# A new order of all work behind the third attention step, up to block 2

## The chip, the cores and the metric

The kernel runs on one core of one Trainium2 chip. The metric is device time in microseconds (us) of one execution; the time given is the median of three runs. A profile was taken of one further execution.

## The reference

Three stages follow one another: a retention attention (no softmax, a decay between positions), a gated expert layer, and a soft mixture of experts whose slots are a softmax over all tokens.

```
scores = scale * q @ k.T                       # 8 batches, 8 heads, 576 positions, 64 wide
attn = (scores * Dmat) @ v                     # Dmat: gamma_h ** (i - j) where i >= j
x = attn, heads side by side                   # 4608 tokens x 512
h = x @ moe_w_in                               # 512 x 2048
x = (h * sigmoid(1.702 * h)) @ moe_w_out       # 2048 x 512
logits = x @ phi                               # 32 slots
d = softmax of logits over tokens              # slot_input = d.T @ x
slot_out[e] = relu(slot_input[e] @ w1[e]) @ w2[e]
out = softmax of logits over slots @ slot_out
```

## The kernel before

The tokens go in 12 blocks of 384, and a block in three attention steps of 128 tokens; 36 steps in all, nine to a pair of sequences. Attention carries a running state in PSUM (St), so a step is made of three kinds of 64x64 matmuls: its outputs, what it adds to the state, and the scores of the next step. A block's tokens then meet 16 slices of the first expert matrix (M, twelve 128x128x384 matmuls each, three for every 128 of depth: high weight by high x, high weight by low x, low weight by high x), a gate on ACT (g), and a 32x32 transpose on DVE (t).

All engines work through their instructions in the order in which the program writes them (a manual schedule). Blocks 0 and 1 and the attention steps up to 8 are written out as a string START of tokens (lines 49 to 62), which line 827 runs one by one; blocks 2 to 11 follow in a loop. The tokens, each with its engine:

- SP (DMA issues): T load of a step (1 MB), W and O load of a slice of the first expert matrix and of the turned second one (0.5 MB each), C and K constants, N four DMAs that shuffle a quarter of half a block's transposed gates into the tile nat (line 412). N0 to N7 are block 0, N8 on are block 1.
- PE: B, A, P, Q, R products of attention (line 227; B scores alone, P outputs and scores, Q outputs, R states, A all three), D a matmul whose result nobody reads (line 569), M expert products (line 368), e the product of phi with two turned slices (line 336), L logits (line 419), lt and dp parts of the softmax, SG the sum over a block's tokens into the slots (line 479).
- ACT: ua and aa (line 304), h (the high part of a weight slice, line 323), g (line 378), xh (the high part of x, line 252).
- DVE: us, as (line 308), uc, ac (line 313), v (the low part of a slice, line 327), SC, SS, xs (lines 237, 241, 245), t (line 394), ed (line 340), xl of steps 0 to 2 (line 257).
- POOL: KN (line 233) and xl from step 3 on.

Within products(), own matmuls (states, then scores) and outputs are issued in turn, on different halves of the rows. Three PSUM tiles (tag "r") are shared by outputs, scores, e and SG; three (tag "h") by M and D. The raw slices W and O go through seven places, six of them the tile early_raw, which shares its room with nat: the first N can't start before the last raw slice of O has been read by its ac. An ac of slice i writes place i % 4 of a ring that e of slices i - 4 has read. SG0 needs all of N0 to N7 landed, and the part dp0 of the softmax. Step 2 was done as Q2 (outputs) and, two products later, R2 (states). The token G runs one gate instruction early; it read St and wrote into early_raw.

```
        for i in range(max(len(own), len(out_))):
            for what, turn in ((own, 0), (out_, 1)):
                if i < len(what):
                    o, w, a, b, p, j, first_ = what[i]
```

Of the kernel before, what the change touches and what calls it, by code (L numbers as in the profile page):

```python
# [12 lines left out]
AF = mybir.ActivationFunctionType  # L13
# [5 lines left out]
B, H, S, D = 8, 8, 576, 64  # L19
# [7 lines left out]
C = 64  # L27
# [7 lines left out]
NDC = DM // 128  # L35
# [11 lines left out]
PC = NP * CP  # L47

START = (
# [13 lines left out]
).split()  # L63

RAWS = 7
# [68 lines left out]
def tile_kernel(ctx, tc, qkv, w_in, w_turned, w_out, phi, w1, w2, consts, out):  # L134
# [52 lines left out]
    xh, xl = {}, {}  # L187
# [16 lines left out]
    def products(g, parts=("out", "state", "score")):  # L204

        n, cb = g + 1, g % NPB
        own, out_ = [], []
        if "out" in parts and g >= 0:
            t = packs[g]
            Op = Ops[g] = ps.tile([128, NP, NSEQ, C], F32, tag="r", name="Op", bufs=3)  # L210
            for p, j in pairs:
                if cb:
                    out_.append((Op, t, SS, QT, p, j, True))
                out_.append((Op, t, VN, SC, p, j, cb == 0))
        if "state" in parts and g >= 0 and (g == 0 or 0 < cb < NPB - 1):
            own += states(g)
        if "score" in parts and n < NSTEP:
            Sp = Sps[n] = ps.tile([128, NP, NSEQ, C], F32, tag="r", name="Sp", bufs=3)
            own += [(Sp, packs[n], KT, QT, p, j, True) for p, j in pairs]
        if "state" in parts and cb == NPB - 1 and 0 <= g < NSTEP - 1:  # L220
            own += states(n)
# [4 lines that stand above are left out]
                    for h, oh in ((lo, (lo, hi)[turn]), (hi, (hi, lo)[turn])):  # L226
                        pe.matmul(o[oh, p, j, :], w[h, a, p, j], w[h, b, p, j], start=first_, stop=True,  # L227
                                  skip_group_check=True)
# [133 lines left out]

    def expert_scores(n, fc):
        hp = hps[n, fc] = ps.tile([128, NB], F32, tag="h", name="hp", bufs=3)
        i = 0
        for dc in range(NDC):
            for a, b in ((0, xh), (0, xl), (1, xh)):
                pe.matmul(hp, wt[fc][:, a, dc, :], b[n][:, dc, :], start=(i == 0), stop=(i == 3 * NDC - 1))  # L368
                i += 1

    def gelu(n, fc):
        g, fl = divmod(fc, GF)
# [193 lines left out]
    def again():  # L566
# [9 lines left out]
        "aa": lambda i: bring_sign(f"O{i}"), "as": lambda i: shift_low(f"O{i}"),  # L576
        "ac": lambda i: join(f"O{i}", ring[:, i % 4]), "e": wp_product, "ed": wp_turn,
        "A": products, "B": lambda i: products(i - 1, ("score",)), "P": lambda i: products(i, ("out", "score")),
        "Q": lambda i: products(i, ("out",)), "R": lambda i: products(i, ("state",)),
        "KN": scale_keys, "SC": scale_scores, "SS": scale_state,  # L580
        "xs": scale_out, "xh": x_high, "xl": lambda i: x_low(i, dve if i < STEPS else pool),
        "M": lambda i: expert_scores(*divmod(i, NFC)), "g": lambda i: gelu(*divmod(i, NFC)),
# [5 lines left out]
    def step(x):  # L588
        if x == "C":
            sp.dma_start(cs, consts[:, 128:128 + NCS])  # L590
        elif x == "K":
            constants()
        elif x == "D":
            again()
        elif x == "G":
            act.activation(early_raw[0:1, 0, 0:1], St[0][0:1, 0, 0, 0:1], AF.Gelu_apprx_sigmoid)
        elif x == "Z":
            dve.tensor_copy(sum4r, st.pop("s4"))
        else:
            name = x.rstrip("-0123456789")  # L600
            what[name](int(x[len(name):]))
# [351 lines left out]
```

## Time and profile before

| | |
|---|---|
| median of 3 runs | 650.64 us (649.29 to 652.19) |
| profiled execution, its own time | 650.49 us |
| its span, first to last instruction | 648.6 us |
| PE busy | 626.7 us (97%) |
| DVE, ACT, POOL busy | 293.8, 216.7, 77.6 us |
| mean rate of DMA | 232 GB/s |
| granted TensorE clock | 0.994 of full |

The span is 1.9 us shorter than the execution's time. The busy share of PE says that it has work almost all the time, not that it works at its peak. START takes the first 120 us of the span.

### The profile page before, as it was taken

How to read it: one execution, taken by the hardware profiler on the slowest of the kernel's cores; microseconds unless marked ns; L12 is line 12 of the kernel's file. 1: busy time of each engine (PE TensorE's matmuls, PEld its weight loads, DVE VectorE, ACT ScalarE, POOL GpSimd, SP SyncE). 2: the span in 40 equal slices, each digit the busy share in tenths (PEclk: the TensorE clock that was granted, in tenths of full speed). 3: DMA queues.
4: the chain of work that ended last, by engine and by line, in shares of the span. 5: the costliest groups of instructions: out<-in, count | busy, mean ns of one | idle time of the engine just before them, and what ended most of it. 6: DMA issues, size and time to landing. Idle time of an engine off the chain costs nothing.

```text
span 648.6 us, 19162 instructions
## 1 busy us (share of the span) xinstructions
PE 626.7 (97%) x8439; PEld 538.0 (83%) x8439; DVE 293.8 (45%) x581; ACT 216.7 (33%) x409; POOL 77.6 (12%) x70
## 2 busy tenths in 40 slices
PE   6999999999999999999999999999999999999994
PEld 6898788898998989989989979989898798874562
DVE  4989933364453443454534534544535323123043
ACT  2765432141242232422412412412424224231042
POOL 2011101211112101121111011111121100001000
PEclk9999999999999999999999999999999999999997
DMA  8997657687676756746657657566566777999998
GB/s 337 404 329 267 256 109 218 164 215 187 174 265 165 195 187 163 211 141 180 172 163 182 183 145 187 170 158 179 179 176 190 251 204 209 413 361 421 412 414 353
DMA packets 62546, 150.64 MB, mean 232 GB/s; under 512 B 8192, under 2 KB 42368, under 8 KB 53248
## 3 DMA queue, kind: packets, MB, share of 16 engines
q1 hardware_dynamic: 62464, 149.43, 72.8%
q8 instruction: 66, 1.08, 0.7%
q14 instruction: 16, 0.13, 0.1%
HBM read 101.16 MB, written 13.63 MB: 177 GB/s over the span
## 4 chain that ended last, share of the span: by engine, by line
PE 87%; DMA 6%; DVE 3%; ACT 1%; issue 1%; POOL 0%; SPq 0%; DVEq 0%; ACTq 0%
PE hp L368 56%; PE Lg L419 5%; PE Sg L479 4%; PE Sp L227 4%; PE St L227 4%; DMA early_raw<-in_moe_w_in_dram 3%; PE Op L227 2%; PE h_ps L710 2%; PE op L787 2%; PE so_ps L761 1%; DMA early_raw<-in_w_turned_dram 1%; PE so_ps L753 1%; DMA ring<-in_w_turned_dram 1%; DMA pack<-in_qkv_dram 1%; PE tpg L401 1%
## 5 line engine op out<-in xcount | busy, mean ns | idle before, releaser
L368 PE MATMUL hp<-x,w 128*128 128x384 f32 x2304 | 420.0, 339 | 1.6 <-POOL x L257 1.3
L368 PEld LDWEIGHTS hp<-x,w 128*128 128x128 f32 x2304 | 397.4, 188 | 20.2 <-issue 15.7
L394 DVE STREAM_TRANSPOSE pre<-gT 128x384 f32<-128x384 f32 x172 | 95.3, 569 | 165.5 <-ACT gT L378 154.5
L378 ACT ACTIVATE gT<-hp 128x384 f32<-128x384 f32 x188 | 91.1, 490 | 232.6 <-PE hp L368 232.2
L257 POOL TENSOR_TENSOR x<-xs,x 128x512 fp32r<-128x512 f32 x33 | 42.5, 1288 | 310.6 <-ACT x L252 310.6
L227 PE MATMUL Op<-pack 64*64 64x64 f32 x2176 | 71.8, 220 | 0.2 <-issue 0.2
L227 PEld LDWEIGHTS Op<-pack 64*64 64x64 f32 x2176 | 66.8, 135 | 0.6 <-issue 0.6
L252 ACT CAST x<-xs 128x512 fp32r<-128x512 f32 x36 | 22.3, 620 | 87.5 <-DVE xs L245 87.4
L233 POOL TENSOR_TENSOR pack<-pack,cs 128x512 f32<-128x512 f32 x30 | 32.2, 1072 | 126.9 <-DMA pack<-in_qkv_dram 111.3
L227 PE MATMUL Sp<-pack 64*64 64x64 f32 x1152 | 41.3, 222 | 5.6 <-DMA pack<-in_qkv_dram 5.5
L227 PEld LDWEIGHTS Sp<-pack 64*64 64x64 f32 x1152 | 37.8, 138 | 8.1 <-DMA pack<-in_qkv_dram 5.5
L237 DVE TENSOR_TENSOR pack<-Sp,cs 128x512 f32<-128x512 f32 x36 | 24.7, 686 | 33.5 <-PE Op L227 25.8
L227 PEld LDWEIGHTS St<-pack 64*64 64x64 f32 x1024 | 33.2, 137 | 7.4 <-issue 7.3
L227 PE MATMUL St<-pack 64*64 64x64 f32 x1024 | 37.4, 224 | 0.0
L419 PE MATMUL Lg<-gT,Wp 128*32 128x384 f32 x376 | 36.3, 493 | 0.5 <-DVE Lall L466 0.5
L479 PE MATMUL Sg<-nat,dn 128*32 128x512 f32 x264 | 30.4, 593 | 0.0
L245 DVE TENSOR_TENSOR xs<-Op,cs 128x512 f32<-128x512 f32 x36 | 24.5, 681 | 3.1 <-PE Op L227 3.1
L241 DVE TENSOR_TENSOR pack<-St,cs 128x512 f32<-128x512 f32 x32 | 21.8, 680 | 3.4 <-PE St L227 2.0
L304 ACT ACTIVATE early_raw<-early_raw 128x512 f32<-128x512 f32 x28 | 18.9, 685 | 12.3 <-DMA early_raw<-in_moe_w_in_dram 6.3
L479 PEld LDWEIGHTS Sg<-nat,dn 128*32 128x32 f32 x264 | 8.4, 110 | 17.1 <-issue 16.9
L485 DVE SCALAR_TENSOR_TENSOR acc<-acc,corr,Sg 128x512 f32<-128x512 f32 x10 | 7.5, 748 | 28.1 <-PE Sg L479 28.1
L419 PEld LDWEIGHTS Lg<-gT,Wp 128*32 128x32 f32 x376 | 9.6, 109 | 11.9 <-issue 9.1
(142 smaller groups left out, 386.8 us busy)
## 6 DMA issues: line engine op xcount, KB each, us to landing
pack<-in_qkv_dram SPq DMA_DIRECT2D x36, 1024.0 KB, 6.2
nat<-pre SPq DMA_DIRECT2D x352, 96.0 KB, 2.2
wx<-in_moe_w_dram SPq DMA_DIRECT2D x19, 1024.0 KB, 11.2
ring<-in_moe_w_out_dram SPq DMA_DIRECT2D x16, 512.0 KB, 4.0
early_raw<-in_moe_w_in_dram SPq DMA_DIRECT2D x15, 512.0 KB, 6.7
early_raw<-in_w_turned_dram SPq DMA_DIRECT2D x13, 512.0 KB, 6.9
wx<-in_moe_w_dram SPq DMA_DIRECT2D x11, 512.0 KB, 10.1
out_dram<-wx SPq DMA_DIRECT2D x5, 1024.0 KB, 7.5
```

The lines of the kernel that those rows point to most:

```text
L227: pe.matmul(o[oh, p, j, :], w[h, a, p, j], w[h, b, p, j], start=first_, stop=True, skip_group_check=True)
L233: (dve if n in (3, 4) else pool).tensor_tensor(k, k, by_state(ksc[:, n % NPB, :]), op=ALU.mult)
L237: dve.tensor_tensor(packs[n][:, SC], Sps.pop(n), across(dtab), op=ALU.mult)
L241: dve.tensor_tensor(packs[n][:, SS], St[n // NPB], by_state(stsc[:, n % NPB, :]), op=ALU.mult)
L245: dve.tensor_tensor(xss[g], Ops.pop(g), across(osc), op=ALU.mult)
L252: act.copy(xh[b_][:, :, i * CP:(i + 1) * CP], xss[g].rearrange("p a j c -> p a (j c)"))
L257: (eng or pool).tensor_tensor(xl[b_][:, :, cols_], xss.pop(g).rearrange("p a j c -> p a (j c)"), xh[b_][:, :, cols_], op=ALU.subtract)
L368: pe.matmul(hp, wt[fc][:, a, dc, :], b[n][:, dc, :], start=(i == 0), stop=(i == 3 * NDC - 1))
L378: act.activation(gT[n, g][:, fl, :], hps.pop((n, fc)), AF.Gelu_apprx_sigmoid)
L394: dve.transpose(pre[n, hf][:, :, :, fh, :].rearrange("p c b i -> p (c b) i"), gT[n, g][:, fl, :].rearrange("p (x j) -> p x j", j=32))
L419: pe.matmul(Lg[n][32 * fl:32 * fl + 32, :], Wp[:, g * GF + fl, :], gT[n, g][:, fl, :], start=(g == 0), stop=(g == NFC // GF - 1))
L479: pe.matmul(Sg[32 * b:32 * b + 32], dn[n][:, c, :], nv[:, 4 * b:4 * b + 4], start=(c == 0), stop=(c == NT128 - 1))
```

## The change

The string START holds the same tokens in another order, with one exception: Q2 and R2 become one token S2, so that step 2's outputs and states are issued in turn. Every load, every DVE, ACT and POOL instruction and every matmul stays. What moves: S2 and the scores B3 stand ahead of M0, with two D ahead of S2 and one behind B3; W0 and W1 stand behind T2 as before, but G no longer holds them, since it now reads and writes gate_room (set by a memset on POOL); the transposes t and the slices O stand in another order; e, L, products and softmax parts stand in longer runs between the M's; N0 stands behind T7 and is followed by T8; SG0 and A8 stand three M's earlier against the rest. The very first expert product, M0, takes its twelve matmuls by terms: four of high weight by high x, four of low weight by high x, four of high weight by low x.

```diff
--- before.py
+++ after.py
@@ -47,19 +47,19 @@
 PC = NP * CP
 
 START = (
-    "T0 C T1 T2 B0 KN0 SC0 R0 G SS1 P0 KN1 W0 W1 R1 SC1 T3 W2 xs0 W3 KN2 SS2 P1 xh0 W4 W5 xl0 SC2 T4 ua0 W6 xs1 Q2 D "
-    "D D us0 ua1 us1 xh1 uc0 xs2 h0 xl1 xh2 v0 xl2 W7 uc1 h1 ua2 M0 KN3 v1 us2 ua3 R2 g0 uc2 h2 W8 us3 M1 v2 ua4 uc3 "
-    "us4 h3 ua5 uc4 W9 M2 g1 v3 h4 us5 W10 SS3 KN4 K ua6 B3 v4 g2 uc5 W11 ua7 M3 us6 h5 us7 uc6 ua8 v5 h6 uc7 W12 M4 "
-    "g3 v6 h7 us8 O0 ua9 v7 ua10 uc8 W13 M5 g4 SC3 h8 us9 ua11 v8 uc9 ua12 W14 M6 Z us10 g5 us11 h9 uc10 aa0 v9 h10 "
-    "A3 uc11 O1 T5 g6 v10 h11 us12 O2 ua13 us13 v11 M7 ua14 SC4 W15 SS4 uc12 aa1 M8 uc13 g7 us14 h12 xs3 h13 uc14 xh3 "
-    "v12 M9 g8 v13 O3 h14 us15 as0 ua15 v14 aa2 M10 uc15 g9 as1 h15 as2 ac1 ac0 A4 T6 g10 as3 aa3 O4 ac2 O5 ac3 O6 "
-    "M11 v15 O7 SC5 KN5 O8 SS5 O9 xl3 xs4 g11 t0 M12 xh4 as4 aa4 t1 xl4 aa5 t2 t3 e1 e0 ed1 g12 as5 as6 M13 aa6 ed0 "
-    "ac5 aa7 as7 ac4 ac7 g13 ac6 M14 t4 KN6 t5 t6 aa8 as8 L0 A5 xs5 t7 g14 xh5 xl5 t8 aa9 as9 t9 M15 t10 T7 O10 t11 "
-    "O11 SC6 O12 e2 SS6 g15 O13 e3 O14 t12 ed2 M16 ac8 ed3 O15 ac9 t13 t14 g16 KN7 t15 M17 aa10 as10 ac10 aa11 as11 "
-    "g17 ac11 M18 aa12 as12 aa13 as13 L1 e4 g18 ed4 ac12 ac13 M19 e5 ed5 aa14 as14 ac14 aa15 as15 ac15 g19 M20 N0 e6 "
-    "g20 ed6 N1 M21 e7 g21 ed7 N2 M22 N3 L2 L3 g22 M23 sp0 lt0 g23 M24 t16 t17 A6 t18 t19 t20 t21 M25 T8 SS7 g24 N4 "
-    "N5 N6 N7 SC7 xs6 dp0 t22 g25 M26 xh6 t23 xl6 M27 g26 A7 g27 L4 L5 SS8 T9 SC8 M28 xs7 xh7 xl7 g28 M29 KN9 g29 M30 "
-    "SG0 A8 g30 M31 t24 xs8 t25 xh8 SC9 xl8 g31 t26 t27 t28 t29 t30 t31 N8 T10 N9 N10 N11 "
+    "G T0 C T1 B0 T2 KN0 SC0 R0 P0 KN1 KN2 SS1 R1 W0 xs0 SC1 SS2 W1 xh0 xl0 P1 ua0 D us0 SC2 xs1 uc0 ua1 D us1 xh1 "
+    "T3 S2 h0 uc1 xl1 xs2 xh2 B3 W2 W3 D W4 h1 ua2 ua3 v0 us2 xl2 v1 uc2 W5 W6 h2 W7 M0 g0 us3 uc3 h3 us4 ua4 M1 v2 "
+    "v3 uc4 M2 t0 us5 h4 v4 ua5 g1 g2 uc5 W8 M3 us7 us6 h5 ua6 v5 ua7 T4 W9 KN3 uc6 SS3 h6 uc7 M4 SC3 h7 v6 us8 ua8 "
+    "W10 g3 v7 g4 M5 g5 uc8 ua10 A3 M6 ua9 W11 us10 us9 xs3 M7 t1 h8 O0 ua11 O1 g6 us11 uc9 v8 h9 M8 v9 uc10 aa1 "
+    "W12 K h10 g7 uc11 W13 SS4 SC4 xh3 us12 T5 h11 v10 aa0 v11 W14 ua12 M9 KN4 ua13 M10 ua14 as0 g8 as1 ac0 us13 "
+    "W15 uc12 uc13 ac1 t7 A4 us15 h12 KN5 g9 us14 uc14 e0 h13 ua15 ed0 O2 v12 as2 aa2 O3 g10 SC5 v13 M11 O4 h14 g11 "
+    "aa3 M12 uc15 g12 as3 M13 xl3 v14 ac3 T6 h15 SS5 aa4 O5 ac2 O6 M14 xs4 O7 v15 e1 as5 O8 aa5 A5 Z aa7 O9 xh4 as4 "
+    "xl4 ac4 as7 aa6 M15 xs5 O10 ac5 xh5 ed1 ac7 O11 as6 ac6 g13 g14 O12 t2 e2 t4 t3 L0 g15 e3 t5 xl5 O13 as10 as11 "
+    "M16 O14 g16 M17 g17 aa8 as8 aa14 ac8 M18 O15 t8 g18 M19 as9 t11 T7 ed3 as13 ed2 M20 t14 SC6 as14 aa10 aa11 SS6 "
+    "t10 M21 aa12 KN6 as12 ac11 as15 g19 M22 t12 aa15 ac10 aa9 ac9 e5 t6 ac14 aa13 ac15 e4 L1 g20 ed4 e7 KN7 g21 "
+    "ed5 ac12 ac13 A6 ed7 SS7 M23 SC7 t15 M24 t9 t13 g22 M25 e6 g23 N0 xs6 T8 L2 ed6 g24 L3 N1 xh6 sp0 A7 lt0 M26 "
+    "xs7 xl6 N2 SS8 SC8 g25 N3 g26 M27 N4 M28 T9 N5 M29 t16 KN9 dp0 t21 t23 A8 N6 t17 t18 g27 t22 xh7 xs8 L4 N7 t19 "
+    "t24 g28 g29 t20 SG0 t27 xl7 N8 L5 t29 M30 xh8 T10 N9 N10 g30 M31 g31 xl8 t30 t28 SC9 N11 t26 t25 t31 "
 ).split()
 
 RAWS = 7
@@ -362,11 +362,11 @@
 
     def expert_scores(n, fc):
         hp = hps[n, fc] = ps.tile([128, NB], F32, tag="h", name="hp", bufs=3)
-        i = 0
-        for dc in range(NDC):
-            for a, b in ((0, xh), (0, xl), (1, xh)):
-                pe.matmul(hp, wt[fc][:, a, dc, :], b[n][:, dc, :], start=(i == 0), stop=(i == 3 * NDC - 1))
-                i += 1
+        terms = [(a, b, dc) for dc in range(NDC) for a, b in ((0, xh), (0, xl), (1, xh))]
+        if (n, fc) == (0, 0):
+            terms.sort(key=lambda x: x[0] + 2 * (x[1] is xl))
+        for i, (a, b, dc) in enumerate(terms):
+            pe.matmul(hp, wt[fc][:, a, dc, :], b[n][:, dc, :], start=(i == 0), stop=(i == 3 * NDC - 1))
 
     def gelu(n, fc):
         g, fl = divmod(fc, GF)
@@ -576,7 +576,7 @@
         "aa": lambda i: bring_sign(f"O{i}"), "as": lambda i: shift_low(f"O{i}"),
         "ac": lambda i: join(f"O{i}", ring[:, i % 4]), "e": wp_product, "ed": wp_turn,
         "A": products, "B": lambda i: products(i - 1, ("score",)), "P": lambda i: products(i, ("out", "score")),
-        "Q": lambda i: products(i, ("out",)), "R": lambda i: products(i, ("state",)),
+        "S": lambda i: products(i, ("out", "state")), "R": lambda i: products(i, ("state",)),
         "KN": scale_keys, "SC": scale_scores, "SS": scale_state,
         "xs": scale_out, "xh": x_high, "xl": lambda i: x_low(i, dve if i < STEPS else pool),
         "M": lambda i: expert_scores(*divmod(i, NFC)), "g": lambda i: gelu(*divmod(i, NFC)),
@@ -593,7 +593,8 @@
         elif x == "D":
             again()
         elif x == "G":
-            act.activation(early_raw[0:1, 0, 0:1], St[0][0:1, 0, 0, 0:1], AF.Gelu_apprx_sigmoid)
+            pool.memset(gate_room[0:1, 0:1], 0.0)
+            act.activation(gate_room[0:1, 1:2], gate_room[0:1, 0:1], AF.Gelu_apprx_sigmoid)
         elif x == "Z":
             dve.tensor_copy(sum4r, st.pop("s4"))
         else:
```

## Rows read from the trace of the kernel before

**Rows 1.** Page, parts 1 and 5: busy us, share, count; mean ns

```profile
PE 626.7 (97%) x8439; PEld 538.0 (83%) x8439; DVE 293.8 (45%) x581; ACT 216.7 (33%) x409; POOL 77.6 (12%) x70
...
L419 PE MATMUL Lg<-gT,Wp 128*32 128x384 f32 x376 | 36.3, 493 | 0.5 <-DVE Lall L466 0.5
```

**Rows 2.** Windows: length, busy PE, PEld, DVE, ACT, POOL, clock, DMA share, GB/s

```profile
60.00:80.00 20.00, 18.38 (x339) 15.63 (x338) 18.14 (x39) 9.57 (x18) 2.45 (x2) 1.00 0.68 256
```

**Rows 3.** Waits of PE, 0 to 125 us: total, times, longest

```profile
PE hp L368 <- POOL x L257: 1.3, 2, 0.9
PE wps L336 <- issue: 1.1, 1, 1.1
PE wps L336 <- DVE xs L245: 0.7, 1, 0.7
PE wps L336 <- DVE pack L237: 0.5, 1, 0.5
```

**Rows 4.** Timeline of PE, 13 to 32 us: start, us, line, tiles, count

```profile
13.14 3.07 PE L227 MATMUL Op<-pack 64*64 64x64 f32 x98 [0.24 <-issue]
16.14 2.20 PE L569 MATMUL again<-pack 128*128 128x384 f32 x6
...
18.80 2.18 PE L368 MATMUL hp<-x,w 128*128 128x384 f32 x11 [0.29 <-DVE x L257]
20.91 1.15 PE L227 MATMUL St<-pack 64*64 64x64 f32 x32
21.99 4.43 PE L368 MATMUL hp<-x,w 128*128 128x384 f32 x24
...
27.43 4.78 PE L368 MATMUL hp<-x,w 128*128 128x384 f32 x26
```

**Rows 5.** Timeline of PE, four M in a row; one M between two e

```profile
37.98 8.59 PE L368 MATMUL hp<-x,w 128*128 128x384 f32 x48
...
78.50 0.65 PE L336 MATMUL wps<-ring,phis 128*32 128x64 f32 x32
79.09 2.35 PE L368 MATMUL hp<-x,w 128*128 128x384 f32 x12
81.37 0.65 PE L336 MATMUL wps<-ring,phis 128*32 128x64 f32 x32
```

**Rows 6.** Window of the products A4 alone, columns as in rows 2

```profile
46.50:48.52 2.02, 2.02 (x129) 1.95 (x128) 0.00 (x0) 0.00 (x0) 1.64 (x2) 1.00 0.81 312
```

**Rows 7.** Timeline of SP, 81 to 109 us: N0-N3, T8, N4-N7, T9

```profile
81.74 11.33 SPq L412 DMA_DIRECT2D nat<-pre  x16
95.50 0.34 SPq L184 DMA_DIRECT2D pack<-in_qkv_dram  x1
95.88 12.75 SPq L412 DMA_DIRECT2D nat<-pre  x16
108.74 0.54 SPq L184 DMA_DIRECT2D pack<-in_qkv_dram  x1
```

**Rows 8.** Timeline of DVE: the last ac before N0

```profile
81.03 0.69 DVE L313 SCALAR_TENSOR_TENSOR ring<-early_raw 128x512 int32<-128x512 int32 x1
```

**Rows 9.** DMA, 81.7 to 108.7 us: instruction queue; issues, KB, us to landing

```profile
q8 instruction: 3, 0.05, 0.8%
...
nat<-pre SPq DMA_DIRECT2D x32, 96.0 KB, 2.8
```

**Rows 10.** Line 412, 78 to 130 us: duration of one issue, min/median/max ns

```profile
L412 SPq DMA_DIRECT2D nat<-pre x49: 585/598/1982, 81.7 to 129.9; - x49
```

**Rows 11.** Timeline of PE: SG0, then the first M of block 2

```profile
112.10 2.78 PE L479 MATMUL Sg<-nat,dn 128*32 128x512 f32 x24
...
119.80 8.42 PE L368 MATMUL hp<-x,w 128*128 128x384 f32 x47 [0.43 <-POOL x L257]
```

**Rows 12.** Timeline: an as on DVE beside an xl on POOL

```profile
67.53 1.42 DVE L308 TENSOR_SCALAR early_raw<-early_raw 128x512 int32<-128x512 int32 x1
...
67.39 1.27 POOL L257 TENSOR_TENSOR x<-xs,x 128x512 fp32r<-128x512 f32 x1 [8.04 <-ACT x L252]
```

## The prediction

> **What bounds the kernel now.** I read the page first: PE is busy 97% of the span [rows 1], so only two things can move the time, fewer or shorter pieces of PE work and idle time of PE. Next come the waits of PE in the stretch that START covers: behind the first landing they add up to some 3.6 us, 1.3 for the low part of x from POOL and 2.3 in three waits of the e products [rows 3]. From M1 to the end of the first logits there is no other idle time on PE that the waits name. DVE is the engine behind it: 18.14 of 20 us at 60 to 80 [rows 2]. What a busy PE hides is read from its timeline. Four M's in a row take 46.50 - 37.98 = 8.52 us (to the product that rows 6 begin with), an M between two e's 81.37 - 79.09 = 2.28 [rows 5]. With m for an M and s for a change to other work and back, 4m + s = 8.52 and m + s = 2.28, so m = 2.08 and s = 0.20. And step 2 costs its states twice over: the R2 row alone holds PE from 20.91 to 21.99, 1.08 us for 32 records, while A4 gets 128 records through in 2.02 us because two kinds alternate [rows 4, 6].
>
> **The change, part by part.** All work stays, so the sum is a new place for each piece on PE's line, and then a look at what is not ready there.
>
> The head. The row at 13.14 holds 98 records in 3.0 us, 34 of P1 and 64 of Q2, so Q2 starts at about 14.1 and takes 2.0; three D's take 2.05 (2.20 less the overlap of the last end) [rows 4]. P1 comes 0.1 later, since SC1 now stands behind xs0 on DVE. After the change PE runs from 14.2: two D's, S2, B3, one D, M0. S2 has 16 pairs of outputs and 8 of states, 96 records; by the alternation of A4 the states hide and it takes Q2's 2.0. So M0 starts at 14.2 + 2.05 + 2.0 + 1.1 = 19.4. It needs xs2, xh2 and v0: S2 ends at 17.6, and two operations of the 0.69 kind [rows 8] on end give 19.0; the low part of x comes later but M0 wants it only for its last four matmuls, that is what the order by terms is worth (0.3 us of waiting before [rows 4]). Three M's and a change later M3 starts at 25.7. Before it was 27.43 with the same work done [rows 4]: 1.7 us won, of which 1.08 is R2 hidden, 0.4 two changes less, the rest idle time. G's early start lets W0 and W1 leave SP some 7 us sooner, but they queue behind T2 all the same; I cost that at nothing, as M0 waits for x, not for W0.
>
> M3 to e5. Twenty M's at 2.08, A3 to A5 at 2.02 [rows 6], e0 to e3 at 0.59 (79.09 - 78.50) [rows 5], L0 at 36.3/47 = 0.77 [rows 1], and four and a half changes at 0.20: 41.6 + 6.1 + 2.4 + 0.8 + 0.9 = 51.8, so e5 starts at 77.5. The three old waits for e are gone by place: e0 follows A4 alone, with the ac of its slices moved forward on DVE, and e1 comes after M14 rather than M12. What is late next is block 1's x. On DVE, as6 and ac6 (for e3) now stand right beside xl4 and xl5 on POOL, and an as beside an xl has taken 1.42 us where its own length is near 0.4 [rows 12]; also aa7 and as7 stand ahead of xh4 and xs5, so one late slice of O delays x. Bounds: 0 if the slice lands in time, 1.0 to 1.5 if not. I take 0.5, nearer the low end since A5 itself comes two M's sooner against block 0. e5 then starts at 78.0. Before, it started at 78.50 with three M's fewer done [rows 5].
>
> e5 to SG0: here the gain is given back. ac14 must wait for e5 (the ring place that e5 reads), and ac14, ac15, ed4, ed5, ac12, ac13 stand in a row on DVE: 0.6 for e5, then four starts 0.60 apart and two ed of 0.2, so the last raw slice is read at about 81.6, and only then may N0 overwrite early_raw. Before, N0 started at 81.74, right behind the last ac at 81.03 [rows 7, 8]: the shuffles start no earlier than they did. They are 32 DMAs on SP that took 11.33 and 12.75 us; with T8 (0.34) and T9 (0.54) between them that is 24.96 [rows 7]. T8 no longer waits for A6 (2.4 us in the gap from 93.07 to 95.50 [rows 7]), since A6 is done at about 83. So N7 is issued by 106.6, and its last DMA, 0.6 from issue to issue and 2.8 from issue to landing [rows 9, 10], is there at 108.8. PE by itself would be at SG0 sooner. From e5's start: four e's 2.4, L1 to L4 3.1, A6 to A8 6.1, seven M's 14.6, lt0 and dp0 together 0.8 (an estimate, five matmuls beside M's 0.17 each), changes 0.5: 27.5, so 105.5. SG0 waits 3.3 us.
>
> [...] First the rows: one issue of line 412 has a median of 598 ns but went up to 1982, and three packets of the instruction queue fall into the stretch [rows 9, 10]; in the trace they lie at the long issues, so I take those for their price. [...]
>
> SG0 to block 2. SG0 2.7, L5 0.8, M30 and M31 with a change 4.3: block 2 starts at 108.8 + 7.8 = 116.6. Before it started at 119.80 less one matmul, 119.6, as the first M of block 2 waited 0.43 for xl8 [rows 11]; now SG0, L5, M30 and M31 lie between A8 and it, 7.8 us against the one M of before, and xl8 is there in time. Nothing behind START changes and PE has no stall there that isn't tied to PE's own progress, so I carry the difference to the end: 119.6 - 116.6 = 3.0 us. Against the profiled execution's own 650.49 us (0.15 under the median of the three, 650.64) this gives 647.4.
>
> **The rivals.**
>
> One: the shuffles aren't late. At the median issue of 0.60 and 0.04 between, 32 take 20.4; with T8 and T9 N7 would be issued by 102.9 and landed by 105.1, under the 105.5 at which PE comes. SG0 doesn't wait, 3.3 us more are won: 644.1. For it speaks that 0.60 is the usual issue [rows 10]; against it that both old stretches of 16 took 11.33 and 12.75, not 10.2 [rows 7]. Chance 0.2.
>
> Two: block 1's x and e3 are late by the upper bound and a little more (as6 behind POOL, one slice of O late). All that hangs on e5 moves with it, N0 too: 1.5 us more, 648.9. For it speaks rows 12, against it that A5, which x waits for, and M16 move forward together. Chance 0.2.
>
> Three, to the other side: SP's line of shuffles grows. T8 and T9 are now each followed closely by shuffles, and the packets of both share the same DMA engines; should the stretch grow past 24.96 by more than the 3.0 us won, the kernel gets slower. With four issues as long as the longest (4 x 1.4 over the median), and T8 and T9 each holding a later issue for 2 us, it is 20.4 + 0.9 + 5.6 + 4 = 30.9, SG0 starts at 114.7, and the time is 653.3. For it speaks the 12.75 of the stretch that had a T ahead of it against 11.33 without [rows 7], against it that it needs every issue at its worst. Chance 0.08.
>
> Four: the change doesn't do what it says, S2 doesn't hide the states, since only half of S2 alternates. Then 1.08 us come back ahead of everything: 648.5. Against it, P1 has the same shape and alternated. Chance 0.05.
>
> **How the numbers follow.** The forecast, 647.4, has the remaining 0.47, with a range of its own of 646 to 649 (the wait of x 0 to 1.5, the stretch of shuffles 1.2 either way). For the range I leave out half of rival three, the lower edge of rival one and little else: 643.8 to 650.4. Half a per cent, about what a measurement of this kernel can tell from no change, is 3.3 us, so the border of faster lies at 647.4, on the forecast itself. Faster: half of the forecast and rival one, 0.24 + 0.2, and a bit of the others, 0.46. Slower by as much takes 653.9, the far end of rival three: 0.04. The same: 0.5.
>
> **What would show it.** In the trace after: R2's row at 20.9 is gone and M3 starts near 25.7 (27.43 before); S2's 96 records take some 2.0; the e products carry no waits over 0.5 us; e5 starts near 78 behind M22; N0 on SP starts near 81.6, as before; SG0 has an idle time of about 3 us in front that a DMA of nat ended, and starts near 109; the first M of block 2 starts near 116.6 without waiting for POOL. SG0 without a wait shows rival one; a wait of M16 or e3 over 1 us rival two; N0 to N7 taking over 28 us rival three. The forecast is wrong as a whole if A3 or A4 waits: SC3 and the landing of T5 come closest ahead of them, and a wait there moves all behind it.

## The result and the profile after

The changed kernel takes 658.20 us, the median of six runs (656.89 to 658.92); the kernel before takes 650.36 in as many (649.29 to 652.19). The ratio is 1.0115, with a 95% interval of 1.0097 to 1.0133. The forecast was 647.4, the range 643.8 to 650.4: the kernel got 1.15% slower where I had given that 4 in 100. The profiled execution of after took 658.33 us, its span is 656.6.

First its page, part 1, as in [rows 1], and the waits of PE up to the end of START, as in [rows 3].

```profile
PE 626.7 (95%) x8439; PEld 538.5 (82%) x8439; DVE 294.5 (45%) x581; ACT 215.7 (33%) x409; POOL 79.2 (12%) x71
```

```profile
PE Sp L227 <- DMA pack<-in_qkv_dram: 6.8, 2, 5.7
PE Op L227 <- issue: 3.0, 2, 2.8
PE Sp L227 <- issue: 2.2, 2, 1.3
PE Sg L479 <- DMA nat<-pre: 2.1, 1, 2.1
PE wps L336 <- DVE ring L313: 1.9, 2, 1.6
PE hp L369 <- ACT gT L378: 0.6, 1, 0.6
```

PE is busy 626.7 us as before, to the tenth; that is a coincidence, as S2 hides R2's 1.08 us [rows 4] and a stretch at a granted clock of 0.50, shown below, makes other work longer. By the sums, the 7.9 us by which the span grew are idle time of PE. The largest part of that idle time, 3.0 + 2.2 us, has no engine and no DMA as its releaser: "issue", PE waiting for nothing that the profile shows. Where it arises is told by the starts of the first matmuls (us, read from the timeline of PE in both traces):

| | M0 | M3 | M16 | block 2 | block 3 | block 4 | end |
|---|---|---|---|---|---|---|---|
| before | 17.89 | 27.43 | 67.36 | 119.04 | 164.93 | 211.38 | 648.63 |
| after | 23.87 | 30.21 | 71.01 | 126.71 | 173.17 | 219.30 | 656.55 |
| later by | 5.98 | 2.78 | 3.65 | 7.68 | 8.25 | 7.92 | 7.92 |

From block 4 on the difference stands still. All but 0.24 us of it is made in START, most of it in two places: ahead of M0, and between M16 and block 2. (M3 is less late than M0, as R2 and B3 now stand ahead of M0.) The timeline of PE in after shows the first of these places (the same columns as [rows 4]; dots stand for rows of S2 and B3), and the windows show the clock granted there (the third column from the end).

```profile
15.80 1.68 PE L227 MATMUL Op<-pack 64*64 64x64 f32 x34 [2.83 <-issue]
17.41 2.69 PE L569 MATMUL again<-pack 128*128 128x384 f32 x4
...
20.97 1.35 PE L227 MATMUL Op<-pack 64*64 64x64 f32 x32
...
22.23 1.03 PE L227 MATMUL Sp<-pack 64*64 64x64 f32 x29
23.19 0.91 PE L569 MATMUL again<-pack 128*128 128x384 f32 x2
```

```profile
16.00:17.00 1.00, 1.00 (x31) 1.00 (x28) 0.00 (x0) 0.13 (x1) 0.00 (x0) 0.66 1.02 418
17.00:18.00 1.00, 1.00 (x10) 0.79 (x7) 0.48 (x1) 0.00 (x0) 0.00 (x0) 0.50 1.04 422
18.00:19.00 1.00, 1.00 (x3) 0.48 (x2) 1.00 (x3) 0.75 (x2) 0.00 (x0) 0.50 1.01 410
19.00:20.00 1.00, 1.00 (x3) 0.19 (x1) 0.90 (x3) 0.52 (x1) 0.00 (x0) 0.63 1.04 410
20.00:21.00 1.00, 1.00 (x65) 0.97 (x66) 0.55 (x1) 0.00 (x0) 0.00 (x0) 1.00 1.03 406
```

In the middle of P1 PE stands still for 2.83 us. Behind that the granted clock is 0.50 until between 19 and 20 us, and two D's take 2.69 us where [rows 4] has three in 2.20. From 15.80 to the first product of S2, at 20.03, PE needs 4.2 us for 34 products of P1 and two D's; at the pace of [rows 4] (98 products in 3.0 us, three D's in 2.05) it would be 2.4. So the pause costs 2.6 us more than before and the slow clock some 1.8. S2 follows and takes 2.1, from 20.03 to the first product of B3 at 22.12.

Now a view that tells what the "issue" is: windows that start at 0 and end just before PE goes on after each of these pauses. The brackets behind PE and PEld count the matmuls and weight loads that PE has started by then.

```profile
0.00:15.78 15.78, 7.32 (x222) 6.84 (x223) 4.82 (x8) 3.10 (x5) 3.42 (x8) 1.00 0.88 349
0.00:64.60 64.60, 54.25 (x986) 50.21 (x986) 45.69 (x86) 33.08 (x60) 6.06 (x10) 0.97 0.89 330
0.00:90.00 90.00, 77.53 (x1368) 71.21 (x1369) 65.91 (x126) 43.39 (x79) 11.84 (x14) 0.98 0.77 287
0.00:102.33 102.33, 88.93 (x1624) 81.11 (x1624) 69.70 (x133) 46.54 (x84) 13.11 (x15) 0.98 0.78 276
```

The sums of the two counts are 445, 1972, 2737 and 3248; the trace has 4, 13, 16 and 17 more instructions of PE by then that are not counted as busy (most of them semaphores). That makes 449, 1985, 2753 and 3265. So PE pauses behind its instructions 448, 1984, 2752 and 3264, give or take one: 192 plus 1, 7, 10 and 12 times 256. The page of after shows what comes in such pieces:

```profile
q8 instruction: 66, 1.08, 0.7%
```

66 packets of the instruction queue carry 1.08 MB, 16.4 KB each. In both traces they pair off one by one with PE's 66 entries into a piece, so I take this queue to bring PE's program. And each pause ends 2.3 to 2.9 us after such a packet starts (13.29, 62.32, 87.60 and 99.49 us in the trace of after). So my reading is that PE waits for its own program, and that the next piece is asked for at about the time when PE comes to the piece before. Where PE is at M's, 24 instructions each and 8.59 us for four [rows 5], 256 last over 20 us by my estimate; of the 64x64 products a step like A4 has 256, in 2.02 us [rows 6]. Before has the same pause in the same place, 0.24 us at instruction 448: it is the bracket in the first line of [rows 4], and I passed over it. The other "issue" of [rows 3], 1.1 us at an e, falls at instruction 1612 and 5.4 us after a packet, so it is no such pause; what ended it stays open.

The second place, from M16 on. First DVE and POOL around e3, then SP with N0, T8, N1 to N4, T9 and N5 to N8, to be laid beside [rows 7].

```profile
67.42 1.51 DVE L308 TENSOR_SCALAR early_raw<-early_raw 128x512 int32<-128x512 int32 x1
69.03 1.34 DVE L313 SCALAR_TENSOR_TENSOR ring<-early_raw 128x512 int32<-128x512 int32 x1
...
66.90 1.75 POOL L257 TENSOR_TENSOR x<-xs,x 128x512 fp32r<-128x512 f32 x1 [0.96 <-ACT x L252]
68.60 1.22 POOL L233 TENSOR_TENSOR pack<-pack,cs 128x512 f32<-128x512 f32 x1
```

```profile
89.28 3.29 SPq L412 DMA_DIRECT2D nat<-pre  x4
92.68 0.52 SPq L184 DMA_DIRECT2D pack<-in_qkv_dram  x1
93.26 13.43 SPq L412 DMA_DIRECT2D nat<-pre  x16
106.80 0.52 SPq L184 DMA_DIRECT2D pack<-in_qkv_dram  x1
107.36 17.78 SPq L412 DMA_DIRECT2D nat<-pre  x16
```

as6 takes 1.51 and ac6 1.34 beside xl5 and KN6 on POOL, where the medians of their groups are 0.42 and 0.68, and e3 waits 1.56 for them. N0 starts at 89.28, N7's last issue ends at 116.95; A8 waits 1.10 for T9, and SG0, after four of its 24 matmuls, 2.09 for the last shuffles.

### The profile page after: what moved, and what is told of

The parts are those of the page before. It is cut to its first block, busy times and chain, and to the rows that moved or that the text cites. A ratio compares the mean times of both kernels' runs of the same rounds, so it can differ in the third digit from the quotient of the medians.

```text
span 656.6 us, 19163 instructions
## 1 busy us (share of the span) xinstructions
PE 626.7 (95%) x8439; PEld 538.5 (82%) x8439; DVE 294.5 (45%) x581; ACT 215.7 (33%) x409; POOL 79.2 (12%) x71
## 3 DMA queue, kind: packets, MB, share of 16 engines
q8 instruction: 66, 1.08, 0.7%
## 4 chain that ended last, share of the span: by engine, by line
PE 87%; DMA 4%; DVE 3%; SPq 2%; issue 2%; ACT 1%; DVEq 0%; ACTq 0%
PE hp L369 56%; PE Lg L419 5%; PE Sg L479 4%; PE St L227 4%; PE Sp L227 4%; DMA pack<-in_qkv_dram 3%; PE Op L227 3%; PE h_ps L711 2%; SPq L412 2%; PE op L788 2%; DMA early_raw<-in_moe_w_in_dram 1%; PE so_ps L762 1%; PE so_ps L754 1%; DVE ring L313 1%; PE tpg L401 1%
## 5 line engine op out<-in xcount | busy, mean ns | idle before, releaser
L227 PE MATMUL Op<-pack 64*64 64x64 f32 x2176 | 73.5, 221 | 3.0 <-issue 3.0
L227 PEld LDWEIGHTS Sp<-pack 64*64 64x64 f32 x1152 | 37.9, 137 | 10.8 <-DMA pack<-in_qkv_dram 7.0
## 6 DMA issues: line engine op xcount, KB each, us to landing
wx<-in_moe_w_dram SPq DMA_DIRECT2D x19, 1024.0 KB, 13.5
```

## The experiments

Three causes were to be told apart: PE's own program (and with it the early W0 and W1, which are on the DMA queues when a packet is due, and S2, which puts more small matmuls in a row), the order of the tail (A8, SG0 and the shuffles), and e3 beside POOL. The ratio is to before in the same rounds. The last column is the difference to before of the first M of block 4, in the one profiled execution of each; it need not be a typical one (that of e2_free is the slowest of its eight, that of e8_late_e3 the fastest of its ten).

| run | us | ratio to before, 95% | block 4 |
|---|---|---|---|
| after | 658.20 | 1.0097 to 1.0133 | +7.92 |
| e1_hold | 657.82 | 1.0084 to 1.0141 | +5.84 |
| e2_free | 652.65 | 1.0014 to 1.0055 | +3.81 |
| e3_s2 | 653.69 | 1.0036 to 1.0068 | +3.10 |
| e4_late | 654.52 | 1.0046 to 1.0093 | +2.48 |
| e5_s2_fill | 656.60 | 1.0063 to 1.0124 | +4.10 |
| e6_late_qr | 657.43 | 1.0082 to 1.0144 | +4.79 |
| e7_after_fill | 660.72 | 1.0113 to 1.0198 | +9.81 |
| e8_late_e3 | 655.74 | 1.0062 to 1.0105 | +2.31 |
| e9_s2_quick | 652.76 | 1.0036 to 1.0061 | +1.62 |
| e10_before_quick | 651.63 | 1.0010 to 1.0041 | +0.20 |
| e11_late_e3_quick | 656.48 | 1.0089 to 1.0122 | +6.34 |
| e12_hybrid | 655.62 | 1.0073 to 1.0105 | +4.55 |

**e1_hold**: after, with the old G behind R0, so that W0 and W1 are held again.

```diff
-    "G T0 C T1 B0 T2 KN0 SC0 R0 P0 ...
+    "T0 C T1 B0 T2 KN0 SC0 R0 G P0 ...
-            pool.memset(gate_room[0:1, 0:1], 0.0)
-            act.activation(gate_room[0:1, 1:2], gate_room[0:1, 0:1], AF.Gelu_apprx_sigmoid)
+            act.activation(early_raw[0:1, 0, 0:1], St[0][0:1, 0, 0, 0:1], AF.Gelu_apprx_sigmoid)
```

> The changed kernel, but G reads St and writes early_raw as it did before, so W0 and W1 leave SP only behind the first products. Theory A (the 2.8 us pause of PE inside P1 and the half clock behind it come from W0 and W1 lying in the DMA queues ahead of the packet that brings PE's next instructions): that packet starts near 10.7 instead of 13.3, the pause falls to 0.4 or less, PEclk stays 1.00 from 16 to 20 us, M0 starts near 19.5 (23.9 in the changed kernel) and M3 near 25.8; time 653.9 (653.2 to 654.6). Rival B (the pause comes from the new order of DVE in front of P1, SC1 behind xs0, or from the two D's and S2): pause and clock stay, time 657.5 to 658.5.

657.82 us, no gain that the medians show, and a time in the rival's range. The rival's reason does not hold all the same: the packet of P1 came at 10.87 instead of 13.29, and the pause there is gone, with nothing changed on DVE. But a new one stands inside S2, at instruction 704, and M0 starts only 0.56 us sooner than in after:

```profile
20.41 0.37 PE L227 MATMUL Op<-pack 64*64 64x64 f32 x2 [2.42 <-issue]
```

```profile
0.00:20.39 20.39, 12.03 (x350) 10.63 (x350) 7.81 (x13) 4.53 (x7) 3.33 (x7) 1.00 0.89 337
```

**e2_free**: the kernel before with nothing but the new G at the start, W0 and W1 free.

```diff
-    "T0 C T1 T2 B0 KN0 SC0 R0 G SS1 P0 ...
+    "G T0 C T1 T2 B0 KN0 SC0 R0 SS1 P0 ...
```

> The kernel before, with nothing changed but G: it gates a memset cell at the very start, so W0 and W1 leave SP behind T2 at about 3 us. Theory A: the pause inside P1 grows from 0.4 to about 2.8 us, PE falls to the half clock behind it, M0 ends 3 to 4.5 us later; time 653.4 to 655. Rival B: no such pause, W0 lands a little sooner, time 650.4 as before.

652.65 us, ratio 1.0034: what I had costed at nothing costs by itself 2.2 us by this ratio and 3.8 in the profile. The packet for the piece behind 448 starts at 13.62, not 10.67 (below, the queue in before from 10.5 to 10.8 us and here from 13.5 to 13.7), and P1 stands still as in after:

```profile
q8 instruction: 1, 0.02, 22.7%
...
q8 instruction: 1, 0.02, 30.0%
```

```profile
15.94 4.54 PE L227 MATMUL Op<-pack 64*64 64x64 f32 x98 [3.00 <-issue]
```

**e3_s2**: the kernel before with S2 in the place of Q2, without R2.

```diff
-... ua0 W6 xs1 Q2 D D D ... M0 KN3 v1 us2 ua3 R2 g0 ...
+... ua0 W6 xs1 S2 D D D ... M0 KN3 v1 us2 ua3 g0 ...
```

> The kernel before with one edit: Q2 and R2 become S2, where Q2 stood; all else keeps its order. If the states hide behind the outputs as the prediction had it, R2's 1.08 us and one change of 0.2 leave PE's line ahead of M1 and nothing comes back but the stalls at e1, e0, e3 and M16, which depend on DVE and DMA and may take it all: 649.1 if nothing is taken back, 650.4 if the later stalls grow by as much. If they do not hide, 650.4 with no gap closed at M1.

653.69 us, ratio 1.0052, where I had expected a gain or nothing. The 32 matmuls and 32 weight loads that S2 adds pull instruction 704 from R2 (behind M0 in before) to the end of S2, where the packet, which starts at 17.20 as it did in before (16.99), is late. The pause is 3.33 us, and the D's behind it run at a lower granted clock (0.50 from 21 to 23 us):

```profile
19.55 0.33 PE L227 MATMUL Op<-pack 64*64 64x64 f32 x2 [3.33 <-issue]
19.81 3.77 PE L569 MATMUL again<-pack 128*128 128x384 f32 x6
```

**e4_late**: e1_hold with A8, SG0 and N8 three M's later, as they stood before.

```diff
-... dp0 t21 t23 A8 N6 ... xh7 xs8 L4 N7 ... t20 SG0 t27 xl7 N8 L5 t29 M30 xh8 T10 N9 N10 g30 M31 g31 ...
+... dp0 t21 t23 N6 ... xh7 L4 N7 ... t20 t27 xl7 L5 t29 M30 A8 xs8 xh8 M31 SG0 N8 T10 N9 N10 g30 xl8 g31 ...
```

> As e1_hold, and A8 (with xs8, xh8) moved between M30 and M31, SG0 (with N8) behind M31. Theory C (the shuffles N0 to N7 and T9 come too late for A8 and SG0 where the change put them, which cost 1.1 us in front of A8 and 2.1 to 2.7 at SG0): those waits go and the time is 3 us under e1_hold, 650.6 to 651.2. Rival D (what is won there is lost behind, since N8 to N15 of block 1 start later and SG1 waits for them, or x of block 2 is late): within 0.7 us of e1_hold.

654.52 us, 3.3 under e1_hold. The waits of A8 and SG0 are gone. So these places in the tail cost 3.3 us, and some 4.5 are left (ratio 1.0070). In the profile e3 waits 1.57, and the stops at instructions 704, 1984 and 3264 (S2, A5, A7) have 1.59, 0.55 and 1.27. Part of the gain is given back one block later: block 2 starts 1.47 us behind before, block 3 2.80, as dp of block 1, which is done among the M's of block 2, waits 1.1 for DVE's dT.

**e5_s2_fill**: e3_s2 with 48 dummy products of zeros (192 instructions, 64 columns) ahead of B0.

```diff
+        elif x == "F":
+            pool.memset(gate_room[0:64, 0:64], 0.0)
+            t = ps.tile([128, NB], F32, tag="h", name="fill", bufs=3)
+            for _ in range(48):
+                pe.matmul(t[0:64, 0:64], gate_room[0:64, 0:64], gate_room[0:64, 0:64], start=True, stop=True)
```

> The kernel of e3_s2 with 48 matmuls of 64x64 on a zeroed tile put ahead of B0, in the time in which PE waits for its first load (192 records more, weight loads counted; their result is read by nobody). Theory A2 (PE's instructions come in pages of 256 records; a page is asked for when PE enters the one before it, and where products run through a page in some 4 us under a full DMA queue the next one is not there): the ends of pages move 192 records forward, so the one inside S2 (record 704, a stall of 3.3 us) falls on the end of P1 instead and is asked for earlier; the stall inside S2 goes, 0.5 to 1.5 us may appear near record 704 in front of S2, PEclk stays 1.00 at 18 to 22 us; time 650.0 to 651.5. Rival B2 (S2 waits for its own inputs, scores and states of step 2): the stall of 3.3 us stays where it is in S2; time 653.7.

656.60 us: a miss, by a flaw of the experiment. The dummies ran until 11.1 us, 5.5 past the landing of T0, and B0 waited for them:

```profile
0.93 10.39 PE L599 MATMUL fill<-gT 64*64 64x64 f32 x95 [0.93 <-POOL gT L596]
```

The stops in P1 and S2 were gone, as expected of the shift, and M0 started at 22.76, no later than in e3_s2 (22.80) though B0 started 5.4 us later. The time itself decides nothing; e9_s2_quick repeats it.

**e6_late_qr**: e4_late with the head of before (Q2, three D, M0, R2, M1, M2, B3, M3).

```diff
-... D us0 SC2 xs1 uc0 ua1 D us1 xh1 T3 S2 h0 uc1 xl1 xs2 xh2 B3 W2 W3 D W4 ... M0 g0 ... M1 v2 v3 uc4 M2 t0 ...
+... us0 SC2 xs1 uc0 ua1 us1 xh1 T3 Q2 D D D h0 uc1 xl1 xs2 xh2 W2 W3 W4 ... M0 R2 g0 ... M1 v2 v3 uc4 M2 B3 t0 ...
```

> The kernel of e4_late with the head of the kernel before: S2 apart again into Q2 ahead of M0 and R2 behind M0, three D's behind Q2, B3 behind M2; all else in the changed order. Theory A2: 64 records less stand between the end of a page and the first M's, the stall in S2 (1.6 us) and the half clock behind it go, R2 costs its 1.08 again; M3 starts near 27.4 as before; time 652.3 (651.5 to 653.2). Rival: the products cost the same wherever they stand and the head loses the 1.3 of R2 and its changes: 655.8.

657.43 us, 2.9 over e4_late: a miss of 5 us. The stop in the head is gone, but M3 starts at 28.94, against 27.61 with S2 and its stop of 1.59. Q2 waits 0.42 for SC2 and M0 0.42 for x, because DVE's line is still that of after; P0 and R1 took 0.6 us longer than in e4_late, with the same instructions in both; the rest is R2. For the 0.6 there is a sign in the traces: their first entry of the granted clock, 1.00, stands at 9.67 us in e4_late and at 11.63 here, and products ahead of that moment are slower (32 in 1.98 us for B0 in before) than behind it (32 in 1.15 for R2 [rows 4]). Why it comes later here stays open. Without it the head with S2 is still some 0.6 us ahead, with the stop of 1.59 in it; so S2 by itself is a gain, which e3_s2 hid.

**e7_after_fill**: after with 40 of the dummies of e5_s2_fill (160 instructions).

> The changed kernel, W0 and W1 still early, with 40 matmuls of 64x64 on a zeroed tile ahead of B0 (160 records more, read by nobody). Theory A2: the ends of pages fall at records 448, 704 and 960 still, which are now the end of R1, the first third of S2 and M0; the page of 448 is asked for before W0 and W1 leave SP, so the pause of 2.8 us in P1 goes; that of 704 is asked for some 2 us sooner against the work, so at most 1.5 us are left in S2; time 654.5 (653.5 to 656). Rival B (the pause in P1 belongs to P1's place and inputs): it stays, 658.2.

660.72 us, no gain where I had expected 3.7. Here too the dummies ran too long, until 9.3. But the places tell: pauses of 0.23, 1.88, 1.04, 0.81 and 1.15 us stand at instructions 448, 704, 960, 2240 and 3008, counted with the dummies, all 192 + 256k. What stood in A5 in after would be at 2144 now, and A5 has no pause; the e behind it has one, at 2240.

```profile
0.00:26.70 26.70, 22.67 (x477) 20.60 (x477) 11.51 (x20) 7.26 (x12) 3.47 (x9) 1.00 0.84 326
0.00:68.74 68.74, 63.39 (x1113) 59.46 (x1114) 49.85 (x91) 35.49 (x64) 11.17 (x13) 1.00 0.87 323
```

**e8_late_e3**: e4_late with e3 behind M18 instead of behind L0.

```diff
-... t2 e2 t4 t3 L0 g15 e3 t5 xl5 O13 as10 as11 M16 O14 g16 M17 g17 ... M18 O15 t8 g18 M19 ...
+... t2 e2 t4 t3 L0 g15 t5 xl5 O13 as10 as11 M16 O14 g16 M17 g17 ... M18 O15 t8 g18 e3 M19 ...
```

> The kernel of e4_late with one product moved: e3 behind M18 instead of in front of M16. Theory E (e3 waits 1.57 us for ac6, because as6 and ac6 on DVE took 1.5 and 1.3 us beside xl5 and KN6 on POOL): the wait goes, nothing takes its place but the 0.2 of a change more; time 653.1. Rival: M16 waits for xl5 in e3's place and gets most of it back: 654.2.

655.74 us; its runs scatter over 5.5 us, so beside e4_late the medians decide nothing, and the profile, at the lower end of them, is 0.8 shorter. The wait of e3 is gone there. The trace is worth more than the time: M3 starts at 27.57 in spite of a stop of 1.35 in S2, and M16 1.42 us **sooner** than before, 0.65 of it because e3 is still to come. Then block 2 starts 0.29 later and block 3 2.63 later. Four us go between M16 and block 3; measured from M18, which starts 2.58 sooner, it is 5.2. The waits of PE name nearly all of these: e3 itself 0.65, the stop in A7 1.27, e7 0.33 for DVE, L4 0.90 right behind dp0 (DVE's Lall), a step's load 0.69, and dp of block 1 1.69 for dT, less 0.43 that before waits in this stretch. DVE was not short of time in the two longest of its waits; ahead of dp0 it stood idle for 4 us:

```profile
107.74 0.26 DVE L463 COPY dn<-dp 128x96 f32<-128x96 f32 x1 [4.05 <-PE dp L461]
```

And ahead of dT it waited 1.71 for shuffles to land and 2.26 for ACT.

**e9_s2_quick** and its control **e10_before_quick**: e3_s2, and the kernel before, with 56 shorter dummies (16 columns, both halves of the rows in turn; 224 instructions).

```diff
+            for j in range(56):
+                s = slice(64 * (j % 2), 64 * (j % 2) + 64)
+                pe.matmul(t[s, 0:16], gate_room[s, 0:64], gate_room[s, 0:16], start=True, stop=True)
```

> The kernel of e3_s2 (before, with S2 in the place of Q2 and R2) with 56 small 64x64 products of zeros, read by nobody, ahead of B0, while PE has nothing but the landing of T0 to wait for; each has 16 columns, not 64 as in e5_s2_fill, where the dummies ran until 11.1 us and made B0 late. They add 224 records (matmuls and weight loads), so that PE's 448th and 704th record fall where the 224th and 480th fell, and the 960th among the M's. Theory A (PE stops at every 256th record from 448 on when its next piece of program has not come in yet): the stop of 3.3 us inside S2 is gone, some 0.5 us at most is left in P1, M0 starts at 17.9 as before, R2 costs nothing, and the kernel takes 649 to 650, against 653.7 of e3_s2. Rival (S2 costs its 3 us by itself: by its banks, or by an x that comes late): a wait of 2 to 3 us stays in the head wherever the records fall, 652.5 to 654.

> The control of e9_s2_quick: the kernel before with the same 56 small products ahead of B0, and nothing else. Theory A: its only stop at a 256th record is 0.24 us, so it gains at most some 0.3 us from that, 649.8 to 650.6, and a later stop moves to another place. If the dummies help by themselves (PE busy ahead of B0), it shows here: B0 and R0 in under their 1.97 us each, up to 1 us less, 649.3. Rival of both: the dummies hold back B0 as in e5_s2_fill, then B0 starts past 5.6 and the kernel takes over 651.

652.76 and 651.63 us. In both B0 started at 6.93, behind the dummies and 1.4 late. In the control's profile this is all but made good later (block 4 +0.20), but that execution is one of its faster ones: the median is 1.6 over before, as its last rival had it (B0 past 5.6, over 651). So e9_s2_quick is to be laid beside its control, 1.1 us above it. In e9_s2_quick the stop left S2 and a smaller one stands in P1, where instruction 704 is now:

```profile
6.93 1.95 PE L227 MATMUL Sp<-pack 64*64 64x64 f32 x32
8.67 1.92 PE L227 MATMUL St<-pack 64*64 64x64 f32 x32
...
15.73 0.56 PE L227 MATMUL Op<-pack 64*64 64x64 f32 x13 [1.17 <-issue]
```

```profile
0.00:15.71 15.71, 13.50 (x350) 13.13 (x351) 4.56 (x7) 2.06 (x3) 3.48 (x8) 1.00 0.79 297
```

The time lies in the range of the rival, the places do not: M3 starts at 28.52, and at 28.89 in the control. Even with 1.17 us of stop S2 is ahead, so it is not S2 itself that costs 3 us; that rival falls. But M16 starts at 69.19, against 67.88. PE won, and then waited: L0 1.12 us for a Wp of DVE, an e 0.24 longer than in the control. DVE in turn had waited for a slice of O, which it did not in the control:

```profile
59.90 0.47 DVE L308 TENSOR_SCALAR ring<-ring 128x512 int32<-128x512 int32 x1 [1.34 <-DMA ring<-in_w_turned_dram]
```

My 649 to 650 missed that. The dummies didn't make B0 or R0 faster (1.95 and 1.92).

**e11_late_e3_quick**: e8_late_e3 with 32 of the short dummies (128 instructions).

> The kernel of e8_late_e3 (after, with W0 and W1 held, A8, SG0 and N8 three M's later, e3 behind M18) with 32 small products ahead of B0: 128 records, so that the stops at 704 (S2), 1984 (A5) and 3264 (A7) move by 128 records. Theory A: those of 1.35, 1.12 and 1.27 us at S2, A5 and A7 leave their places; from the time that PE takes for the 256 records ahead of each, new ones of 1 to 2.5 us are to be expected in A4 (record 1728), at most 0.5 in the head, and under 1 in A6 and A7 each: 1 to 2 us under e8's profile in all, which started the first M of block 3 2.6 us later than the kernel before. Rival (each of these stops has its own cause at its place): they stay in S2, A5 and A7.

656.48 us. A5 and A7 have no stop any more, and e0, right behind A4, and an e behind A5 have one of 1.52 and 1.47, at instructions 1728 and 2240:

```profile
53.53 0.43 PE L336 MATMUL wps<-ring,phis 128*32 128x64 f32 x15 [1.52 <-issue]
...
69.30 0.36 PE L336 MATMUL wps<-ring,phis 128*32 128x64 f32 x11 [1.47 <-issue]
```

The places came as foretold, the one behind A5 and the head not: there 2.53 us stand at instruction 704, inside S2, since the packet came at 17.12 for a piece that PE wanted earlier than in e8; the granted clock was 0.50 behind it, from 19.8 to 23.2 us. With A7 waiting 1.87 for T8 besides, the sum is worse, not 1 to 2 us better.

**e12_hybrid**: e8_late_e3 up to M18, then what is left (O15 and g18 first) in the order of before.

```diff
-... M18 O15 t8 g18 e3 M19 as9 t11 T7 ed3 as13 ed2 M20 ...
+... M18 O15 g18 KN6 t6 t8 aa9 as9 t9 t10 T7 t11 SC6 SS6 e3 t12 ed2 ed3 ac9 t13 t14 KN7 t15 aa10 ... L1 e4 ...
```

> The order of e8_late_e3 (after, with W0 and W1 held and e3 moved behind M18) up to M18, then what is left in the order of before: e3, L1, e4 and so on, N0 behind M20, T8 and N4 behind M25, A8 and SG0 behind M30. In the profile of e8 M16 started 1.4 us sooner than in before and the first M of block 3 2.6 us later, so 4 us went between M16 and block 3. Theory: they went on after's order of the tail (A6 to A8, L and the softmax close behind one another, shuffles late, block 2's softmax behind them). With before's tail the 1.4 us are kept, less what the stop of 1.1 to 1.3 us at PE's 1984th record (A5) still costs and is counted in them: block 3 starts 1 to 1.5 us sooner than in before, and the kernel takes 648.6 to 649.2 where before takes 650. Rival (the shuffles are bound by DVE's last ac and by SP, not by PE's order: then PE, being 1.4 us early, only waits longer): SG0 or the first M of block 2 waits as much as was won, and the kernel takes 650 to 650.5. If it is over 652, neither holds.

655.62 us: neither theory, as its last sentence puts it. M16 starts 1.16 us sooner than before, M18 2.3 sooner (with e3 still to come), and then L1 waits, and behind that wait the granted clock falls to 0.50 once more, from 77.4 to 80.8 us:

```profile
76.95 1.37 PE L419 MATMUL Lg<-gT,Wp 128*32 128x384 f32 x8 [3.63 <-DVE Wp L340]
```

```profile
78.00:79.00 1.00, 1.00 (x36) 0.93 (x28) 1.00 (x4) 0.00 (x0) 0.00 (x0) 0.50 0.17 66
```

ed3, which writes that Wp, stands behind ten instructions on DVE. DVE waits 1.12 us for ACT at 71.8 and works without a break from there to ed3. My reading of the reason is what DVE had left. Summed over the durations of START's DVE instructions that had not started when M18 did, before has 26.8 us of work left at 72.80; after 33.7 at 75.27, e8_late_e3 33.5 at 70.22, e12_hybrid 33.4 at 70.49. The new order reaches M18 with some 7 us more of DVE's work undone. Here L1 pays for it. In e8_late_e3, with as much left, little was waited for at DVE's line (0.33 by e7), since after's tail asks for its results later; so the work left is a debt only where the order that follows calls it in.

No version was faster than the kernel before.

## Why the prediction was wrong, point by point

**The head.** I had M3 start at 25.7; it started at 30.21. The step that failed is the first one, "PE runs from 14.2": PE stood still 2.83 us in P1 and then ran from 16.3 to 19.7 us at a granted clock of 0.50. The sentence behind it is "I cost that at nothing" on W0 and W1: the cover that I named, T2, was not what mattered. With W0 and W1 on the queues the packet that I take to bring PE's program started some 3 us later (13.29, against 10.67 in before), and e2_free shows the price without anything else. Pause and slow clock, 2.6 + 1.8 us, make up the 4.5 by which M0 (23.87, forecast 19.4) and M3 came late. The other step, S2 in "Q2's 2.0", was right (2.1 us in after; the R2 row is gone) and the gain is there when the stop is set aside: e8_late_e3 has M3 at 27.57 with 1.35 of stop in it, so 1.2 of the 1.7 us that I had summed. But S2 costs a stop of its own (e3_s2), which no term had.

**The packets of [rows 9]** had the answer in them. I took them for the price of SP's issues alone, as they lie at the long ones [rows 9, 10], and never asked which engine's program they bring. By the pairing above the three are pieces of PE's, 256 instructions in 16.4 KB each, and not of SP's, which has 693 instructions in the whole execution. PE passes most of the ends of these pieces without a stop that the waits name: of the 13 at instructions 448 to 3520 it stopped at one in before, for 0.24 us, and at four in after. In the 64x64 products it stood up to 3.33 us (e3_s2). That long issues of SP stand at the three packets (at 91.3, 95.9 and 104.1 us in before, of 1.14, 1.32 and 1.98 us) is so; why, stays open.

**M3 to e5** came to 55.6 us where I had 52.3. e3 waited 1.56, not 0.5: an as slow beside POOL as in [rows 12] (1.51 us here, 1.42 there), at rival two's size. A5 stopped 1.30 us at instruction 1984, where e1 and A5 bring 320 instructions close together; M11 waited 0.6 for ACT. "Wrong as a whole if A3 or A4 waits": it was A5, for a reason that was not on the list.

**e5 to SG0.** N0 started 3.51 us after e5; I had 3.6. The line of shuffles, 24.96 us by my sum, took 27.67. That is one half of rival three's mechanism: T8 and T9 each held a later issue, for 1.38 and 1.08 us, where the rival had 2. Its other half did not come; the 32 issues took 22.21 us in all, against 22.18 before. PE needed 30.2 from e5 to SG0 instead of 27.5; of the 2.7 more, 0.20 are a stop in A6, 0.93 one in A7, 0.33 a wait of e7 and 1.10 that for T9. So SG0 waited 2.09 and not 3.3. e4_late shows that these places cost 3.3 us: both ends of the wait, A8 for T9 and SG0 for N7, stand three M's too early. I had priced the wait and missed that the order before did not have one at all.

**Behind START** the difference is carried to the end, as I said, but for the 0.24 up to block 4, and block 2's first M no longer waits for POOL. Of the 10.1 us by which block 2 came after the forecast's 116.6, 4.5 arose up to M3, 3.3 from there to e5 and 2.3 behind it.

**What I left out altogether** is that the head's gain is PE's only. I read 18.14 of 20 us for DVE at [rows 2] and then costed each piece on PE's line. In e9_s2_quick, e8_late_e3 and e12_hybrid PE comes sooner and gives it back, in waits for what did not come sooner with it: DVE's line in e12_hybrid, a slice of O in e9_s2_quick, and in e8_late_e3 dp0 close ahead of L4, dT behind late shuffles, and stops. What remains open: how much of after's loss each cause has when the others are gone, as the stops move with every change; and why a packet takes about 1 us to start in some places and some 4 in others I only argue, from the loads queued at the time; e1_hold and e2_free test it directly, for W0 and W1 alone.

## What to carry to other kernels

Count PE's instructions, not only its time: a short idle bracket that ended by "issue" inside a run of small matmuls can be a late piece of program (the count tells), a change that puts more small matmuls in a row can make one (3.33 us in e3_s2), and loads on the queues ahead of that piece can make it longer (3.00 in e2_free, 0.24 in before). When an order is changed by hand, compare at a few marks how much work the second engine has left, not only when the first engine gets there. And where one stage is woven closer, ask which transfer was just in time before.

## What the runs showed of the hardware

PE stopped behind its instructions 192 + 256k, in START of before, of after and of ten of the runs, for 0.2 to 3.33 us. In before, after, e2_free, e3_s2 and e11_late_e3_quick it went on 2.3 to 2.9 us after the start of a packet of the instruction queue. Instructions put in ahead moved the places in the work and not the count (e7_after_fill, e11_late_e3_quick). The first such packet started 0.9 us after PE's first instruction of the piece before in before and in e3_s2, and 3.5 and 4.0 us after it in after and e2_free, where W0 and W1 had left SP at about 3 us. The next one, with W's and T's queued, took 3.9 us in before (16.99 behind 13.14), 3.7 in after (19.46 behind 15.80) and 4.0 in e3_s2 (17.20 behind 13.21). Where PE was at M's, packets also started ahead of that instruction (91.17 us against 93.34 in before).

After the stops of 2.42 us (e1_hold), 2.53 (e11_late_e3_quick), 2.83 (after), 3.00 (e2_free) and 3.33 (e3_s2), and after the wait of 3.63 in e12_hybrid, the granted clock was 0.50 for a stretch (in after from 16.3 to 19.7 us). In it two D's took 2.69 us in after, where they would take 1.37 at the pace of [rows 4]. By the estimate above the stop of 2.83 us in after cost 4.4 more than the one of 0.24 in before.
